# Six single PSUM banks for three double ones after the attention, and new latencies in the planner

## The chip, the cores and the metric

The kernel runs on one core of one Trainium2 chip. The metric is device time in microseconds (us) of one execution; lower is better. In the profile PE is the matrix engine (TensorE), PEld its weight loads, DVE the vector engine, ACT the scalar engine, POOL the general-purpose engine (GpSimd), and SP the engine whose queue issues most transfers. L538 is line 538 of the kernel before.

## The reference

Causal attention by blocks of 64 positions, then a feed-forward layer of two matrix products with a leaky ReLU whose slope differs by hidden channel. All data are 32-bit floats.

```python
# q, k, v: 8 batches, 8 heads, 576 positions, 64 channels
scores = scale * np.matmul(q, k.transpose(0, 1, 3, 2))
mask = block_i >= block_j                 # blocks of 64 positions
scores = np.where(mask, scores, -1000000000.0)
attn = np.exp(scores - max); attn = attn / (sum + 1e-09)
x = (attn @ v), as 4608 tokens of 512 channels
h = x @ w_in                              # 512 -> 2048
g = np.maximum(h, 0.0) + alpha * np.minimum(h, 0.0)
out = g @ w_out                           # 2048 -> 512
```

## The kernel before

**Precision.** Each 32-bit operand of the feed-forward layer is split into a high and a low part, and a product is the sum of three matmuls (high by high, low by high, high by low). The attention's matmuls take 32-bit data directly.

**Stages.** The attention goes pair by pair: a pair is two heads of one batch, 32 pairs in all. For each pair PE computes scores (L720) into PSUM, DVE takes row maxima (L725), POOL exchanges them between neighbouring groups of 32 partitions (`swap`, L697), ACT takes exponentials with their sums (L733), DVE transposes (L737), PE multiplies by v (L778), and DVE scales the result into x (L784). In between, six of the sixteen slices of hidden channels are computed for chunks of 256 tokens as they become ready (`chunk_a`): L499 is their first product, L538 their second, and partial sums go to memory. When the attention is done, the remaining ten slices are computed for nine chunks of 512 tokens. There the first product of two slices (`pair1`) is done with seven half-size products (L579) in place of eight, whose sums DVE and ACT build (L588, L592, L597). The last products (L538) add up in four accumulators per chunk, which L878 adds to the partial sums before the store. The weights of these ten slices come as 64-bit floats, or as 32-bit ones where they were converted earlier, and are prepared by DVE, ACT and POOL (L382 to L403, L419); factors of x are formed by DVE and split by ACT with DVE or POOL (L402, L403).

**A product of the first kind.** L499 is issued in three parts of four matmuls each, all into one PSUM bank; other operations can stand between the parts. L579 is issued as one operation of six matmuls into one bank. The bank is then read by ACT (L510, negated ReLU, or L597, a copy) and by DVE (L512, the leaky ReLU's other half; L588 and L592, sums, the latter back into the bank). ACT (L518) or POOL (L516) rounds the result to its high part and POOL subtracts for the low part (L521).

**PSUM.** There are eight banks of 512 floats per partition. Up to the end of the attention three tiles of two banks each, `duo`, hold scores and values, and two tiles of one bank, `bank`, serve the feed-forward work. The attention's last write of x releases an operation of the plan that closes the attention's SBUF pool (`end_attention`); its follower `more_room` then tells the planner that six more slots of the kind `bank` exist. Before the change these are the halves of the three double tiles:

```python
for i in range(2 * DUOS):
    plan.room("bank", 1, lambda slot, i=i: plan.tiles["duo"][i // 2][:, i % 2])
```

Waits between engines are put in by the framework from what each instruction reads and writes; the kernel names none.

**Order.** All work is first collected as operations with an engine, a cost, the buffers that they read and write, and a priority. `Plan.schedule` then simulates the engines: an operation is ready when its inputs are, plus the latency of the engine that made them, and each engine takes the ready operation of lowest priority number for which a buffer is free. The order that comes out is the order in which every engine's instructions are written. Its constants are costs in ns. `LAT` is added after an operation of an engine before others may use its result, `TO_POOL` is added where POOL is the user, `LONGER` stretches costs of DVE, ACT and POOL, and `LAG` shifts the priorities of the feed-forward work during the attention against those of the pairs, which are five units apart:

```python
return 5 * ((t0 + f / of) * CHA * NP / S + LAG)
```

Quotas bound how many banks serve as first products (`hp`) and accumulators (`acc`): one each during the attention, then three and two, later up to five and four.

Of the kernel before, what the change touches and what calls it, by code (L numbers as in the profile page):

```python
# [8 lines left out]
F32 = mybir.dt.float32  # L9
# [7 lines left out]
PSUM = bass.MemoryType.PSUM  # L17
# [18 lines left out]
DUOS, HB, AB, HT, AM, AT, WB = 3, 1, 1, 3, 2, 4, 4  # L36
C0, C1 = -3, 1.5
WARM, WARM_END = 10, 3400
TICK, FULL_COLUMNS, SP0 = 3413.33, 3060, 700
LAG = 7  # L40
VL = 1.0
E0, E1 = -4, 1
NEAR = 12
# [11 lines left out]
SWAP = "POOL"  # L55
# [2 lines left out]
GH, XH, XC = ("ACT", "ACT", "POOL"), "ACT", 2  # L58
LATER = ("DVE", "POOL", "DVE", "POOL", "DVE", "DVE")
GB = 6  # L60
LAT = {"PE": 110, "DVE": 145, "ACT": 135, "POOL": 20}
LONGER = 1.1
QUEUES = ("SP", "ACTQ", "POOLQ")
ISSUE, BEGINS, LANDS, PER_KB, LANES = 430, 1300, 1000, 4.1, 8
TO_POOL = 70


IN_ORDER = {"q", "k", "v", "p", "PTL", "PTH", "z", "r", "R", "raw", "m", "ef", "xb", "X", "xt", "qa", "va", "tail"}
# [16 lines left out]
class Plan:  # L85
# [16 lines left out]
    def op(self, engine, cost, fn, r=(), w=(), prio=0.0, claim=(), then=None, ends=()):  # L102

        i = len(self.ops)
        prio += SHIFTS.get(round(prio, 4), 0.0)
        deps = {j for j, o in enumerate(self.ops) if any(b.kind in ends for b in o[4])} if ends else set()
        for k in r:
            if k in self.writer:
                deps.add(self.writer[k])
        for k in w:  # L110
            if k in self.writer:
                deps.add(self.writer[k])
            deps.update(self.readers.get(k, ()))
        for k in r:
            self.readers.setdefault(k, []).append(i)
        for k in w:
            self.writer[k] = i
            self.readers[k] = []
        bufs = dict.fromkeys(k[0] if isinstance(k, tuple) else k for k in (*r, *w, *claim))
        bufs = [b for b in bufs if isinstance(b, Buf)]  # L120
        for b in bufs:
            b.users += 1
            if b.users == 1 and b.kind in IN_ORDER:
                b.after = self.last.get(b.kind)
                self.last[b.kind] = b
        deps.discard(i)
        self.ops.append((engine, cost, fn, deps, bufs, prio, then))
        return i

    def schedule(self):  # L130
# [43 lines left out]
        while events:  # L174
# [13 lines left out]
            for engine, heap in ready.items():  # L188
# [33 lines left out]
                elif engine in ("DVE", "ACT", "POOL"):  # L222
                    cost *= LONGER
                lat = LAT.get(engine, 0)
                end = t + cost
# [13 lines left out]
                for j in outs[chosen]:  # L239
                    waits[j] -= 1  # L240
                    same = self.ops[j][0] == engine == "PE"
                    more = TO_POOL if self.ops[j][0] == "POOL" else 0
                    ready_at[j] = max(ready_at[j], end + (0 if same else lat + more))
# [57 lines left out]
def attn_ffn(ctx, tc, qT, kT, vT, w_in, w_out, alpha, out):  # L301
# [30 lines left out]
    att = ExitStack()  # L332
    st = att.enter_context(tc.tile_pool(name="st", bufs=1, side="right"))
    ps = ctx.enter_context(tc.tile_pool(name="ps", bufs=1, space=PSUM))

    plan = Plan()
    op = plan.op
    pools = {}

    def rooms(pool, *kinds):  # L340
        for kind, n, shape, dt in kinds:
            plan.room(kind, n, lambda i, kind=kind, shape=shape, dt=dt: (pools[pool] if isinstance(pool, str) else pool).tile(
                [P, *shape], dt, name=f"{kind}{i}"))
# [5 lines left out]
    rooms(xring, ("tail", 1, [NCC, CHA], F32), ("xh", XC, [NCC, CHA], F32R), ("xl", XC, [NCC, CHA], F32R))  # L349
    rooms(fg, ("g", 3, [CHA], F32), ("gh", GB, [CHA], F32R),  # L350
          ("gl", GB, [CHA], F32R), ("o", 2, [DO], F32))
    rooms(ps, ("duo", DUOS, [2, 512], F32), ("bank", 8 - 2 * DUOS, [512], F32))
    plan.quota.update(hp=HB, acc=AB)
    rooms(wa, ("wa", 2 * FA, [2, 512], F32R))

# [1 line left out]
    bank = plan.tiles["bank"][0] = plan.tiles["bank"][0](0)  # L357
# [114 lines left out]
    def turn(t0, f, of):  # L472

        fseq[0] += 1
        if t0 is None:
            return 1.0e6 + fseq[0]
        return 5 * ((t0 + f / of) * CHA * NP / S + LAG)

# [208 lines left out]

    def swap(t, to, of, n, keys, key, scale, pr):

        cost = {"DVE": 75, "POOL": 290, "ACT": 150}[SWAP]  # L690

        def move(a, b):
            o, i = t()[a, to, n], t()[b, of, n]
            if SWAP == "ACT":
                nc.scalar.activation(out=o, in_=i, func=AF.Copy, scale=scale)
            else:
                (nc.vector if SWAP == "DVE" else nc.gpsimd).tensor_scalar(out=o, in0=i, scalar1=scale, scalar2=None, op0=ALU.mult)  # L697
        for i in range(4):
            a, b = slice(32 * i, 32 * i + 32), slice(32 * (i ^ 1), 32 * (i ^ 1) + 32)
            op(SWAP, cost, lambda a=a, b=b: move(a, b), r=keys, w=[(*key, i)], prio=pr)  # L700
        return [*keys, *[(*key, i) for i in range(4)]]

    def scores(src, Ts, pts, z, pr):
# [19 lines left out]
        for t, T in enumerate(Ts):  # L723
            w, o = 32 * (T + 1), off[T]
            op("DVE", c_dve(2 * w), lambda t=t, w=w, o=o: nc.vector.tensor_reduce(  # L725
                out=c()[:, 0, 2 * t:2 * t + 2], in_=sb()[:, :, o:o + w], axis=AX.X, op=ALU.max, negate=True), r=[sb], w=[(c, "n", t)], prio=pr + PM)
        keys = swap(c, 1, 0, slice(0, n), [(c, "n", t) for t in range(len(Ts))], (c, "o"), 0.125, pr + PM)
        op("DVE", 75, lambda: nc.vector.scalar_tensor_tensor(out=c()[:, 2, :n], in0=c()[:, 0, :n], scalar=0.125, in1=c()[:, 1, :n],  # L728
                                                             op0=ALU.mult, op1=ALU.min), r=keys, w=[(c, "m")], prio=pr + PM)
# [10 lines left out]
    def factors_of(z, T0, T1, pr):  # L740

        r, R = Buf("r"), Buf("R")
        ns = slice(2 * T0, 2 * T1)
        keys = swap(z, 1, 0, ns, [(z, "s", T, h) for T in range(T0, T1) for h in range(2)], (z, "o"), 1.0, pr + PZ)
        op("DVE", 80, lambda: nc.vector.scalar_tensor_tensor(out=z()[:, 2, ns], in0=z()[:, 0, ns], scalar=1e-9, in1=z()[:, 1, ns],
                                                             op0=ALU.add, op1=ALU.add), r=keys, w=[(z, "z")], prio=pr + PZ)
        if RCP:
            op("DVE", 150 + 16 * (T1 - T0), lambda: nc.vector.reciprocal(out=z()[:, 1, ns], in_=z()[:, 2, ns]), r=[(z, "z")], w=[(z, "r")], prio=pr + PZ)
        for h in range(2):
            for g in range(2):  # L750
                to, of = slice(64 * h, 64 * h + 64), slice(64 * g, 64 * g + 64)
                on = RCP[2 * h + g] if RCP else "DVE"
                fn = {"POOL": nc.gpsimd.tensor_copy, "ACT": nc.scalar.copy, "DVE": nc.vector.tensor_copy if RCP else nc.vector.reciprocal}[on]
                op(on, {"POOL": 295, "ACT": 150, "DVE": 85 if RCP else 150 + 8 * (T1 - T0)}[on], lambda h=h, g=g, to=to, of=of, fn=fn: fn(
                    out=r()[to, g, T0:T1], in_=z()[of, 1 if RCP else 2, 2 * T0 + h:2 * T1:2]), r=[(z, "r" if RCP else "z")], w=[(r, h, g)], prio=pr + PZ)
        op("DVE", 75 + 67 * (T1 - T0), lambda: nc.vector.transpose(
            out=R()[:, :, 32 * T0:32 * T1].rearrange("p g (t x) -> p g t x", x=32), in_=r()[:, :, T0:T1].unsqueeze(3).to_broadcast([P, 2, T1 - T0, 32])),
            r=[(r, h, g) for h in range(2) for g in range(2)], w=[R], prio=pr + PZ)
        return R
# [81 lines left out]
    def end_attention():  # L841
        att.close()
        pools["wb"] = ctx.enter_context(tc.tile_pool(name="wb", bufs=1, side="right"))

    def more_room():
        rooms("wb", ("w1", 3, [2, 7 * 256], F32R), ("w2", 6, [2, 512], F32R), ("xb", 1, [NCC, CHB], F32), ("X", 2, [2, 512], F32R),
              ("m", 1, [512], F32), ("ws", 1, [512], F32), ("xt", 2, [512], F32), ("g", 4, [CHA], F32))
        for i in range(2 * DUOS):
            plan.room("bank", 1, lambda slot, i=i: plan.tiles["duo"][i // 2][:, i % 2])
        plan.quota["hp"] += HT - HB  # L850
        plan.quota["acc"] += AM - AB

    op("NONE", 0, end_attention, r=xs(B - 1, (1,)), w=["att"], prio=0, then=more_room)
    later_weights(lambda f: 1000 + f)
    def more_sums():
# [71 lines left out]
```

## Time and profile before

| what | value |
|---|---|
| median of 3 runs | 1117.68 us (1116.9 to 1120.61) |
| profiled execution, its time | 1117.85 us |
| its span, first to last instruction | 1116.1 us |
| mean granted clock of PE | 0.986 |
| instructions | 32527 |
| moved by DMA | 119.56 MB, mean 107 GB/s |

A span is the time from the first instruction to the last in one profiled execution; the execution's own time is a little longer. An engine's busy time counts its instructions' durations, without waiting. Matmuls overlap each other, so their mean duration is longer than the distance between two of them. A wait is told as "engine, line, waited for: us in total, times, longest". The granted clock is 1.00 when PE runs at full speed and 0.50 when it is held at half. The profile names a half of a double tile by its tile, `duo`, and leaves buffer numbers out.

### The profile page before, as it was taken

The page shows a single profiled execution, that of the slowest core. Times are in us where ns is not written, and L with a number is a line of the kernel's source. Part 1 is how long each engine was busy: PE and PEld are TensorE (multiplying, and loading weights), DVE is VectorE, ACT ScalarE, POOL GpSimd, SP SyncE. Part 2 cuts the span into 40 slices and gives each one's busy share as a digit, 9 for nine tenths or more (in the row PEclk, how much of TensorE's full clock was granted, in tenths as well). Part 3 has the DMA queues.
Part 4 walks back from the last instruction along what each step waited for, and adds up shares of the span by engine and source line. Part 5 has one row for each costly group of instructions (what it writes and reads, how often), then busy time and mean ns, then how long its engine had stood idle before and what let it go on. Part 6 is the DMA issues. An engine that isn't in the chain of part 4 may idle for free.

```text
span 1116.1 us, 32527 instructions
## 1 busy us (share of the span) xinstructions
PE 1032.5 (93%) x12860; PEld 874.6 (78%) x12860; DVE 762.6 (68%) x1674; ACT 597.1 (53%) x2124; POOL 570.9 (51%) x1018
## 2 busy tenths in 40 slices
PE   6668999999999999999888989999999999999998
PEld 4456777877888888887777878878888888888887
DVE  6998878878777878668766974546555645464452
ACT  6877677767677667565544543324243434343331
POOL 5886545554645556559784763324242424242421
PEclk9988999999999999999899999999999999999999
DMA  9653545546354552324322122121212121212021
GB/s 299 188 173 125 172 161 155 173 152 195 133 168 159 173 160 88 127 80 147 106 95 58 39 77 75 38 76 39 76 38 77 38 76 39 76 38 76 1 76 39
DMA packets 66890, 119.56 MB, mean 107 GB/s; under 512 B 10288, under 2 KB 31024, under 8 KB 66736
## 3 DMA queue, kind: packets, MB, share of 16 engines
q1 hardware_dynamic: 66304, 117.20, 32.1%
q8 instruction: 101, 1.65, 0.6%
q14 instruction: 53, 0.43, 0.1%
q10 hardware_dynamic: 432, 0.27, 0.1%
HBM read 87.04 MB, written 29.36 MB: 104 GB/s over the span
## 4 chain that ended last, share of the span: by engine, by line
PE 71%; DVE 13%; ACT 6%; POOL 5%; issue 4%; DMA 0%; ACTq 0%; DVEq 0%; POOLq 0%
PE duo L538 15%; PE bank L538 14%; PE duo L579 12%; PE bank L499 9%; PE duo L778 7%; PE duo L720 7%; PE bank L579 4%; DVE g L512 3%; PE duo L499 3%; ACT g L510 2%; ACT p L733 2%; DVE duo L592 2%; DVE g L588 1%; DVE c L725 1%; POOL m L397 1%
## 5 line engine op out<-in xcount | busy, mean ns | idle before, releaser
L521 POOL TENSOR_TENSOR gl<-g,gh 128x256 fp32r<-128x256 f32 x288 | 232.2, 810 | 341.2 <-ACT gh L518 292.4
L733 ACT ACTIVATE p<-duo,c 128x256 f32<-128x256 f32 (+8 forms) x576 | 220.2, 408 | 32.8 <-DVE c L728 32.4
L579 PEld LDWEIGHTS duo<-X,w 128*128 128x128 f32 x1332 | 180.4, 190 | 37.4 <-DVE g L588 6.0
L579 PE MATMUL duo<-X,w 128*128 128x256 f32 x1332 | 193.7, 286 | 13.8 <-DVE g L588 4.8
L538 PE MATMUL duo<-w,gh 128*128 128x512 f32 x560 | 178.6, 400 | 10.5 <-DVE g L512 5.5
L518 ACT CAST gh<-g 128x256 fp32r<-128x256 f32 x252 | 101.8, 407 | 134.1 <-PE duo L538 78.5
L697 POOL TENSOR_SCALAR c<-c 32x4 f32<-32x4 f32 (+3 forms) x400 | 97.1, 243 | 93.2 <-DVE c L725 55.3
L725 DVE TENSOR_REDUCE c<-duo 128x2 f32<-128x512 f32 (+8 forms) x288 | 124.9, 479 | 21.1 <-PE duo L720 20.7
L733 ACT ACTIVATION_READ_ACCUMULATOR p<-duo,c 128x1 f32 x576 | 126.2, 219 | 0.0
L538 PE MATMUL bank<-wa,gh 128*128 128x512 f32 x372 | 121.8, 409 | 2.4 <-POOL wa L403 1.1
L499 PE MATMUL bank<-xh,wa 128*128 128x256 f32 x680 | 103.5, 292 | 15.0 <-DVE g L512 7.6
L499 PEld LDWEIGHTS bank<-xh,wa 128*128 128x128 f32 x680 | 89.9, 190 | 34.6 <-DVE g L512 13.9
L538 PEld LDWEIGHTS duo<-w,gh 128*128 128x128 f32 x560 | 92.8, 188 | 29.1 <-DVE g L512 10.3
L592 DVE TENSOR_TENSOR duo<-duo,g 128x256 f32<-128x256 f32 x124 | 52.6, 428 | 89.0 <-PE duo L579 82.1
L737 DVE STREAM_TRANSPOSE PTH<-p 128x576 f32<-128x576 f32 (+4 forms) x160 | 99.1, 630 | 20.6 <-ACT p L733 19.1
L510 ACT ACTIVATE g<-duo 128x256 f32<-128x256 f32 x147 | 55.8, 384 | 104.3 <-DVE duo L592 82.2
L538 PE MATMUL duo<-w,gl 128*128 128x512 f32 x280 | 110.4, 394 | 0.0
L512 DVE SCALAR_TENSOR_TENSOR g<-g,oal,duo 128x256 f32<-128x256 f32 x147 | 69.3, 476 | 51.3 <-ACT g L510 19.8
L510 ACT ACTIVATE g<-bank 128x256 f32<-128x256 f32 x141 | 54.2, 385 | 79.0 <-PE bank L499 52.5
L720 PE MATMUL duo<-k,q 64*32 64x288 f32 (+4 forms) x2560 | 84.4, 372 | 11.3 <-ACT p L733 9.1
L512 DVE SCALAR_TENSOR_TENSOR g<-g,oal,bank 128x256 f32<-128x256 f32 x141 | 66.1, 471 | 28.1 <-ACT g L510 26.8
L579 PEld LDWEIGHTS bank<-X,w 128*128 128x128 f32 x558 | 76.9, 190 | 5.6 <-DVE X L403 0.2
(87 smaller groups left out, 1833.4 us busy)
## 6 DMA issues: line engine op xcount, KB each, us to landing
v<-in_v SPq DMA_DIRECT2D x32, 576.0 KB, 4.0
k<-in_k SPq DMA_DIRECT2D x32, 288.0 KB, 4.2
xb<-xd SPq DMA_DIRECT2D x9, 1024.0 KB, 5.4
m<-part SPq DMA_DIRECT2D x36, 256.0 KB, 3.3
out<-m SPq DMA_DIRECT2D x35, 256.0 KB, 2.1
va<-in_v SPq DMA_DIRECT2D x32, 256.0 KB, 4.8
raw<-in_w_in SPq DMA_DIRECT2D x16, 512.0 KB, 3.6
raw<-in_w_out SPq DMA_DIRECT2D x16, 512.0 KB, 3.9
```

The lines of the kernel that those rows point to most:

```text
L499: nc.tensor.matmul(hp()[:, :n], ww()[:, 0, cc * P:(cc + 1) * P], x()[:, cc, :n], start=(i == 0 and cc == 0), stop=(i == 2 and cc == NCC - 1))
L510: op("ACT", c_act(CHA), lambda: nc.scalar.activation(out=g(), in_=hp()[:, ts], func=AF.Relu, scale=-1.0), r=[hp], w=[g], prio=FP)
L512: op("DVE", c_dve(CHA) + 60, lambda: nc.vector.scalar_tensor_tensor(out=g(), in0=g(), scalar=oal[:, f:f + 1], in1=hp()[:, ts], op0=ALU.mul ...
L518: op("ACT", c_act(CHA, True), lambda: nc.scalar.copy(out=gh(), in_=g()), r=[g], w=[gh], prio=FP)
L521: op("POOL", c_pool(CHA) + 60, lambda: nc.gpsimd.tensor_tensor(out=gl(), in0=g(), in1=gh().bitcast(F32), op=ALU.subtract), r=[g, gh], w=[g ...
L538: nc.tensor.matmul(acc(), a()[:, ts], ww(), start=(first and i == 0), stop=(last and i == 2))
L579: nc.tensor.matmul(bank()[:, :CHA], W()[:, i, 256 * at + P * c:256 * at + P * c + P], B()[:, j, CHA * c:CHA * c + CHA], start=(n == 0), st ...
L697: (nc.vector if SWAP == "DVE" else nc.gpsimd).tensor_scalar(out=o, in0=i, scalar1=scale, scalar2=None, op0=ALU.mult)
L720: nc.tensor.matmul(sb()[32 * i:32 * i + 32, h, off[T]:off[T] + w], q()[hs, qs], blocks(k()[hs], T + 1, 32 * (i % 2)), start=True, stop=True)
L725: op("DVE", c_dve(2 * w), lambda t=t, w=w, o=o: nc.vector.tensor_reduce(out=c()[:, 0, 2 * t:2 * t + 2], in_=sb()[:, :, o:o + w], axis=AX.X ...
L733: op("ACT", 237 + w / 1.2, lambda x=2 * t + h, T=T, h=h, w=w, o=o: nc.scalar.activation(out=pb()[:, 2 * o + h * w:2 * o + h * w + w], in_= ...
L737: op("DVE", 85 + 2.08 * w, lambda to=to, a=a, w=w, o=o: nc.vector.transpose(out=to()[:, a:a + 2 * w], in_=pb()[:, 2 * o:2 * o + 2 * w]), r ...
```

## The change

The pool of PSUM tiles is split: the three double tiles get a pool of their own, `duos`, that is closed together with the attention's SBUF pool. At that point a new PSUM pool, `banks`, is opened, from which the planner's six further `bank` slots are allocated as tiles of one bank each. The number of slots and their kind stay. Beside that, constants of the planner change: the latencies, the stretch, the cost of a swap on POOL, and `LAG`.

```diff
--- before.py
+++ after.py
@@ -37,7 +37,7 @@
 C0, C1 = -3, 1.5
 WARM, WARM_END = 10, 3400
 TICK, FULL_COLUMNS, SP0 = 3413.33, 3060, 700
-LAG = 7
+LAG = 7.25
 VL = 1.0
 E0, E1 = -4, 1
 NEAR = 12
@@ -58,11 +58,11 @@
 GH, XH, XC = ("ACT", "ACT", "POOL"), "ACT", 2
 LATER = ("DVE", "POOL", "DVE", "POOL", "DVE", "DVE")
 GB = 6
-LAT = {"PE": 110, "DVE": 145, "ACT": 135, "POOL": 20}
-LONGER = 1.1
+LAT = {"PE": 240, "DVE": 140, "ACT": 137, "POOL": 95}
+LONGER = 1.06
 QUEUES = ("SP", "ACTQ", "POOLQ")
 ISSUE, BEGINS, LANDS, PER_KB, LANES = 430, 1300, 1000, 4.1, 8
-TO_POOL = 70
+TO_POOL = 85
 
 
 IN_ORDER = {"q", "k", "v", "p", "PTL", "PTH", "z", "r", "R", "raw", "m", "ef", "xb", "X", "xt", "qa", "va", "tail"}
@@ -332,6 +332,7 @@
     att = ExitStack()
     st = att.enter_context(tc.tile_pool(name="st", bufs=1, side="right"))
     ps = ctx.enter_context(tc.tile_pool(name="ps", bufs=1, space=PSUM))
+    duos = att.enter_context(tc.tile_pool(name="duos", bufs=1, space=PSUM))
 
     plan = Plan()
     op = plan.op
@@ -349,7 +350,8 @@
     rooms(xring, ("tail", 1, [NCC, CHA], F32), ("xh", XC, [NCC, CHA], F32R), ("xl", XC, [NCC, CHA], F32R))
     rooms(fg, ("g", 3, [CHA], F32), ("gh", GB, [CHA], F32R),
           ("gl", GB, [CHA], F32R), ("o", 2, [DO], F32))
-    rooms(ps, ("duo", DUOS, [2, 512], F32), ("bank", 8 - 2 * DUOS, [512], F32))
+    rooms(ps, ("bank", 8 - 2 * DUOS, [512], F32))
+    rooms(duos, ("duo", DUOS, [2, 512], F32))
     plan.quota.update(hp=HB, acc=AB)
     rooms(wa, ("wa", 2 * FA, [2, 512], F32R))
 
@@ -687,7 +689,7 @@
 
     def swap(t, to, of, n, keys, key, scale, pr):
 
-        cost = {"DVE": 75, "POOL": 290, "ACT": 150}[SWAP]
+        cost = {"DVE": 75, "POOL": 258, "ACT": 150}[SWAP]
 
         def move(a, b):
             o, i = t()[a, to, n], t()[b, of, n]
@@ -841,12 +843,12 @@
     def end_attention():
         att.close()
         pools["wb"] = ctx.enter_context(tc.tile_pool(name="wb", bufs=1, side="right"))
+        pools["banks"] = ctx.enter_context(tc.tile_pool(name="banks", bufs=1, space=PSUM))
 
     def more_room():
         rooms("wb", ("w1", 3, [2, 7 * 256], F32R), ("w2", 6, [2, 512], F32R), ("xb", 1, [NCC, CHB], F32), ("X", 2, [2, 512], F32R),
               ("m", 1, [512], F32), ("ws", 1, [512], F32), ("xt", 2, [512], F32), ("g", 4, [CHA], F32))
-        for i in range(2 * DUOS):
-            plan.room("bank", 1, lambda slot, i=i: plan.tiles["duo"][i // 2][:, i % 2])
+        rooms("banks", ("bank", 2 * DUOS, [512], F32))
         plan.quota["hp"] += HT - HB
         plan.quota["acc"] += AM - AB
 
```

## The prediction

> **What bounds the kernel now.** I read the page's busy shares first, then the chain of work that ended last, then a table of busy time by stage, then TensorE's groups and its waits after the attention, and last a few microseconds of the timeline.
>
> ```profile
> span 1116.1 us, 32527 instructions
> PE 1032.5 (93%) x12860; PEld 874.6 (78%) x12860; DVE 762.6 (68%) x1674; ACT 597.1 (53%) x2124; POOL 570.9 (51%) x1018
> PE 71%; DVE 13%; ACT 6%; POOL 5%; issue 4%; DMA 0%; ACTq 0%; DVEq 0%; POOLq 0%
> ```
>
> TensorE (PE) is the bound: 93% busy and 71% of the final chain. No transfer is on the chain. The stages differ, so here is the same account by stage; the columns are the stage's length, then busy time and count of PE, weight loads, DVE, ACT and POOL, then the granted clock.
>
> ```profile
> 0.00:101.00 101.00, 67.88 (x1552) 50.78 (x1553) 89.64 (x223) 72.88 (x298) 75.03 (x149) 0.90 0.62 199
> 101.00:495.50 394.50, 382.69 (x7837) 320.26 (x7836) 309.00 (x753) 282.05 (x1239) 211.91 (x566) 1.00 0.46 149
> 495.50:600.00 104.50, 91.31 (x530) 78.66 (x528) 71.20 (x93) 53.05 (x114) 79.70 (x79) 0.97 0.35 114
> 600.00:660.00 60.00, 54.11 (x333) 48.06 (x334) 52.99 (x93) 30.50 (x72) 41.46 (x39) 0.97 0.22 71
> 660.00:1116.10 456.10, 436.49 (x2615) 376.87 (x2613) 239.75 (x517) 158.58 (x403) 162.81 (x187) 1.00 0.16 54
> ```
>
> The attention ends near 495.5 us; until then the double tiles hold scores and values. From there to the end all PSUM banks serve the feed-forward products, six of them as halves of the three old double tiles. In those 620.6 us PE is idle 38.7 us (620.6 minus 91.31, 54.11 and 436.49). The groups of that stretch say where (last columns: busy us, mean ns of one | idle before):
>
> ```profile
> L579 PE MATMUL duo<-X,w 128*128 128x256 f32 x1332 | 193.7, 286 | 13.8 <-DVE g L588 4.8 <-ACT g L510 2.8 <-DVE g L512 1.8
> L538 PE MATMUL duo<-w,gh 128*128 128x512 f32 x560 | 178.6, 400 | 10.5 <-DVE g L512 5.5 <-ACT g L510 2.7 <-DVE duo L592 0.9
> L579 PE MATMUL bank<-X,w 128*128 128x256 f32 x558 | 80.6, 282 | 0.0
> L538 PE MATMUL bank<-w,gh 128*128 128x512 f32 x160 | 50.0, 393 | 0.0
> L499 PE MATMUL duo<-xh,wa 128*128 128x256 f32 x184 | 29.3, 296 | 5.9 <-ACT g L510 5.9
> L499 PE MATMUL duo<-xl,wa 128*128 128x256 f32 x92 | 16.2, 301 | 3.9 <-DVE g L512 3.9
> ```
>
> The same matmul of the same line waits 13.8 us in 1332 when it writes a half of a double tile, and 0.0 us in 558 when it writes one of the two single-bank tiles. So it is for L538 (10.5 us in 560 against 0.0 in 160). Were these waits for a bank to be read and come free, single banks would show them too. One product in the timeline tells what they are:
>
> ```profile
> 554.38 0.64 PE L499 MATMUL duo<-xh,wa 128*128 128x256 f32 x4
> ...
> 555.06 0.38 ACT L510 ACTIVATE g<-duo 128x256 f32<-128x256 f32 x1 [1.33 <-PE duo L499]
> ...
> 555.50 0.74 PE L499 MATMUL duo<-xh,wa 128*128 128x256 f32 x4 [0.47 <-ACT g L510]
> ...
> 556.43 0.47 DVE L512 SCALAR_TENSOR_TENSOR g<-g,oal,duo 128x256 f32<-128x256 f32 x1
> ...
> 556.95 0.74 PE L499 MATMUL duo<-xl,wa 128*128 128x256 f32 x4 [0.71 <-DVE g L512]
> ```
>
> A product of L499 is three parts of four matmuls into one bank. The first part ran at 554.38. The second adds to the same bank, so nothing may yet read that bank, and still it waits until ACT's L510 has read a double tile (0.47 us idle), and the third until DVE's L512 has (0.71 us). What was read can only be the other half. ACT itself had sat idle 1.33 us until the first part ended. So a wait binds the whole double tile: the two products in its halves take turns. L538 shows the same: it adds up into an accumulator, and L510 and L512 never read one.
>
> **The change, part by part.** (1) Six single-bank tiles take the place of the halves: count of tiles, their slots in the planner and all products stay; what goes is the waiting between two halves. PE's waits by stage, as idle us, times, longest; first 495.5 to 600 us:
>
> ```profile
> PE duo L499 <- ACT g L510: 5.9, 9, 2.0
> PE duo L499 <- DVE g L512: 3.9, 6, 0.7
> ...
> PE duo L538 <- DVE g L512: 0.8, 1, 0.8
> ```
>
> then 600 to 660 us:
>
> ```profile
> PE duo L579 <- DVE g L588: 3.0, 3, 1.7
> ...
> PE duo L579 <- DVE duo L592: 1.0, 1, 1.0
> PE duo L579 <- DVE g L512: 1.0, 2, 0.8
> PE duo L579 <- ACT g L510: 0.7, 1, 0.7
> ```
>
> and 660 us to the end:
>
> ```profile
> PE duo L538 <- DVE g L512: 5.5, 10, 1.0
> PE duo L538 <- ACT g L510: 2.7, 6, 0.9
> PE duo L579 <- ACT g L510: 2.0, 7, 0.3
> PE duo L579 <- DVE g L588: 1.8, 3, 0.8
> PE duo L538 <- DVE duo L592: 0.9, 1, 0.9
> PE duo L579 <- DVE g L512: 0.8, 4, 0.2
> ...
> PE duo L538 <- DVE g L588: 0.4, 1, 0.4
> ```
>
> Waits for weights or factors (L403) and for L878 can be the matmul's own and are left out. Idle time understates a stall, because matmuls overlap: one lasts 286 ns, but in an undisturbed run eight start within 0.95 us, one each 119 ns:
>
> ```profile
> 529.34 1.11 PE L499 MATMUL duo<-xh,wa 128*128 128x256 f32 x8
> 530.29 0.64 PE L499 MATMUL duo<-xl,wa 128*128 128x256 f32 x4
> ```
>
> So each wait costs its idle time and 286 minus 119 = 0.167 us more (taken the same for L538, an estimate). By stage: 10.6 us in 16 waits, +2.7 = 13.3 us; 5.7 us in 7, +1.2 = 6.9 us; 14.1 us in 32, +5.3 = 19.4 us. The ceiling is 39.6 us.
>
> What is late next? From 660 us on DVE is busy 239.75 of 456.10 us, POOL and ACT about 160: none needs the time, and I take the whole 19.4. In the first stage PE's floor is its own work; POOL, at 79.70 us, still fits in 104.5 minus 13.3 = 91.2 us. I take the whole 13.3. From 600 to 660 us DVE is busy 52.99 us, and 60 minus 6.9 is 53.1: there DVE (weights and factors of the second part) is late next, at 100%. I take half, 3.4 us, between 0 and 6.9. Sum 36.1 us.
>
> A clock effect hangs on the first stage. A row of the table over a narrower stretch:
>
> ```profile
> 538.50:545.30 6.80, 6.16 (x24) 5.58 (x25) 3.46 (x8) 3.46 (x8) 4.27 (x7) 0.50 0.10 39
> ```
>
> After the longest of those waits (2.0 us) the clock is 0.50 for 6.8 us, which loses up to 3.4 us. It may come back with the wait, or another sparse moment may lose it; bounds 0 and 3.4 us, and I count 0, since 600 to 660 us stays sparse. By the Trainium skill (TensorE: Matmul & The Clock Gate, "HAM oscillation") only idle gaps over some 3.4 us bring the clock down; the trace disagrees, with a drop after 2.0 us of idle between sparse matmuls. By that page's rule this gap isn't the cause, and the sum stays as it is.
>
> (2) The handover: the first matmul into each new tile waits until the double tiles are given back. Their last reader is the last L784, which the planner already awaits before it hands out the halves; what else ends with the attention is already given back at this point. I count 0; the upper bound is one wait of the longest kind above, 2.0 us; a gain is excluded, since no wait goes here.
>
> (3) The planner's numbers. PE's latency goes from 110 to 240 ns, POOL's from 20 to 95, the stretch of the other engines from 1.1 to 1.06, a swap's cost from 290 to 258, LAG from 7 to 7.25. No instruction is added; the written order of all queues changes. How near is 240? Four matmuls at 494.99 would end, at 119 ns each, at 495.47; ACT's reader of that bank begins 0.20 us later:
>
> ```profile
> 494.99 0.64 PE L499 MATMUL bank<-xl,wa 128*128 128x256 f32 x4
> ...
> 495.67 0.39 ACT L510 ACTIVATE g<-bank 128x256 f32<-128x256 f32 x1 [1.29 <-PE bank L499]
> ```
>
> That is nearer to 240 than to 110, so the plan will place readers nearer to where they run. LAG moves the feed-forward work of the attention later by 0.25 x 5 = 1.25 of a pair's 5 units; a pair takes 394.5/32 = 12.3 us, so about 3 us; PE's total work stays, and PE is the bound before and after that point: 0. What the new order brings in the attention, rows can only bound: PE's idle time there is 394.50 minus 382.69 = 11.8 us, the most it can gain. A reordering can as well open waits, so I put the same 11.8 us on the loss side. I take 0, since PE is 97% busy there. The first 101 us, with DVE at 89.64 us, have DVE's weight work as floor: I take 0 again.
>
> **Sum.** The profiled execution took 1117.85 us (span 1116.1), 0.17 us above the median of 1117.68. 1117.85 - 36.1 = 1081.75; I say 1082 us.
>
> **The rivals.** *A half comes back (C).* Without the turns of the halves a product may wait for its own bank: DVE and ACT must do L592, L510 and L512 on a bank before it is free. Against it: the single banks' 0.0 us. For it: PE will come round sooner. L579's 1890 matmuls are 45 pairs of 42; if each pair waited the 0.47 us of the timeline once, 21 us would come back: 1103 us, and with half of that 1092.
>
> *More goes (B).* The order also closes waits in the attention (11.8 us at most), the clock (3.4 us) and the other half of 600 to 660 us (3.5 us) come too: 1082 - 18.7 = 1063 us.
>
> *Nothing goes (E).* The waits are needed ones. By the Trainium skill (PSUM — Partial Sum Buffer, "PSUM bank collisions raise a hardware error") engines are to be kept apart by bank. By that rule a program that guards just so has nothing to lose by sharing a tile, and the waits shown are true ones: 1117.85, within 0.3%. The rows speak against it: no bank is shared at 555.50, and the wait is there.
>
> *Slower (D).* With PE's readers 130 ns later in the plan, the planner slips one more feed-forward block (12 matmuls, 1.43 us) ahead of a pair's scores; on the chip the scores come late, the exponentials after them, and PE runs dry for as long. In all 32 pairs that is 45.8 us: 1128 us. It decides above 36.1 + 3.4 = 39.5 us, that is from 28 of 32 pairs on. Against it: DVE has 309.00 of 394.50 us to do there and can absorb lateness.
>
> **How the numbers follow.** The likeliest case (A): the sum, give or take half of the attention's 11.8 us and the 3.4 us of the middle stage, 9.3 us, rounded outwards: 1071 to 1092 us, chance 0.62. B, 1062 to 1071: 0.15. C, 1092 to 1108: 0.13. E: 0.05. D: 0.05. The range 1064 to 1100 leaves out D, E, half of C and a fifth of B, together 0.2. 0.3% (about 3.4 us) is what a measurement of this kernel can tell from no change. Faster: A, B and C, 0.90; same: E, 0.05; slower: D, 0.05.
>
> **What would show it.** After the attention no row names duo; the L579, L538 and L499 rows on bank have idle times near 0; PE's waits for L510, L512, L588 and L592 fall from 30 us to under 5; the stretch from the attention's end to the end shrinks by some 36 us, about 20 of it behind the stage that has DVE near full. DVE from its stage near 600 us shows as what the chain waits for. The attention still ends at 495 us, give or take 6. I am wrong if that end moves by more than 12 us, if waits on bank rows take the place of those on duo, or if the clock drops in new places.

## The result, and the profile after

The changed kernel takes 0.9692 of the time before (95% interval 0.9662 to 0.9723); the medians are 1084.5 and 1117.3 us. One of the four executions behind the 1084.5 took 2452.88 us, its L581 matmuls 530 ns on average against 282 in the profile below, and does not count in the ratio. In a second comparison, whose first execution gave the profile shown here, the ratio is 0.9681 (0.9657 to 0.9705), 1082.1 against 1118.7 us. The forecast was 1082. Code lines after the change are two higher: L499, L510, L512, L538 and L579 are now L501, L512, L514, L540 and L581.

The head of the page after:

```profile
span 1079.5 us, 32550 instructions
PE 1021.1 (95%) x12860; PEld 876.8 (81%) x12860; DVE 772.0 (72%) x1674; ACT 595.1 (55%) x2124; POOL 570.6 (53%) x1018
```

PE has as many matmuls as before, with 11.4 us less busy time (a matmul that waits inside another's time counts as busy) in a span 36.6 us shorter. Its groups after the attention (486.5 us to the end; mean ns of one | idle before):

```profile
L581 PE MATMUL bank<-X,w 128*128 128x256 f32 x1890 | 261.4, 282 | 6.2 <-DVE g L514 1.5 <-DVE X L405 1.3 <-POOL w L405 1.2
L540 PE MATMUL bank<-w,gh 128*128 128x512 f32 x720 | 225.4, 394 | 0.0
...
L540 PE MATMUL bank<-wa,gl 128*128 128x512 f32 x67 | 28.8, 429 | 6.8 <-POOL gl L523 6.8
L501 PE MATMUL bank<-xl,wa 128*128 128x256 f32 x120 | 19.3, 283 | 0.0
```

No row names duo. The 720 matmuls of L540 have no idle time, where 560 on duo had 10.5 us; L501 has none. What is left is mostly of another kind: 6.8 us for POOL's low part (L523), and waits for weights and factors (L405).

To see where the time went, both profiles are cut at the same points of PE's work: its 2001st matmul, the 9390th (just after the attention), the first L579, the first of the third of nine chunks, and the end. Columns are the stretch and its length, then busy time and count of PE, weight loads, DVE, ACT and POOL, then the granted clock, the busy share of DMA and its GB/s. Before:

```profile
0.00:124.00 124.00, 89.14 (x2001) 67.97 (x2002) 106.00 (x260) 89.33 (x374) 86.86 (x174) 0.92 0.61 197
124.00:496.20 372.20, 362.14 (x7392) 303.64 (x7391) 292.77 (x717) 266.10 (x1167) 200.54 (x541) 1.00 0.45 146
496.20:593.60 97.40, 86.76 (x502) 75.09 (x501) 66.58 (x84) 46.74 (x100) 75.52 (x76) 0.96 0.36 119
593.60:703.90 110.30, 100.69 (x611) 87.14 (x610) 83.83 (x155) 54.05 (x129) 63.76 (x63) 0.98 0.21 68
703.90:1112.50 408.60, 393.76 (x2362) 340.80 (x2360) 212.71 (x459) 140.82 (x358) 144.23 (x166) 1.00 0.15 52
```

After:

```profile
0.00:124.60 124.60, 89.73 (x1998) 67.89 (x2000) 107.85 (x262) 89.85 (x375) 83.62 (x176) 0.82 0.58 196
124.60:496.40 371.80, 365.92 (x7410) 307.42 (x7392) 299.09 (x715) 265.06 (x1167) 206.94 (x545) 1.00 0.47 152
496.40:589.90 93.50, 86.47 (x504) 73.12 (x503) 67.06 (x82) 44.98 (x97) 70.80 (x71) 0.96 0.31 104
589.90:693.10 103.20, 96.98 (x611) 86.00 (x610) 84.09 (x155) 53.54 (x129) 64.92 (x62) 1.00 0.20 68
693.10:1075.20 382.10, 382.03 (x2362) 342.39 (x2360) 213.19 (x459) 141.63 (x358) 144.27 (x167) 1.00 0.16 56
```

The first two stretches are as long as before. The third lost 3.9 us, the fourth 7.1 and the last 26.5: there PE is busy 382.03 of 382.10 us, so its own work is all that is left. The clock of the first stretch is lower, 0.82 against 0.92, and its length is the same within 0.6 us.

### The profile page after: what moved, and what is told of

The parts are those of the page before. It is cut to its first block, busy times and chain, and to the rows that moved or that the text cites. A ratio compares the mean times of both kernels' runs of the same rounds, so it can differ in the third digit from the quotient of the medians.

```text
span 2451.1 us, 32550 instructions
## 1 busy us (share of the span) xinstructions
PE 2432.2 (99%) x12860; PEld 1841.5 (75%) x12860; DVE 757.0 (31%) x1674; ACT 606.6 (25%) x2124; POOL 549.0 (22%) x1018
## 4 chain that ended last, share of the span: by engine, by line
PE 98%; DVE 1%; ACT 1%; POOL 0%; issue 0%; DMA 0%; ACTq 0%; DVEq 0%; POOLq 0%
PE bank L540 42%; PE bank L581 23%; PE bank L501 16%; PE duo L780 9%; PE duo L722 8%; ACT p L735 0%; DVE c L727 0%; POOL c L699 0%; DMA qa<-in_k 0%; DVE PTL L739 0%; DVE xT L786 0%; ACT wa L404 0%; DVE ef L389 0%; DVE m L384 0%; POOL m L399 0%
## 5 line engine op out<-in xcount | busy, mean ns | idle before, releaser
L581 PEld LDWEIGHTS bank<-X,w 128*128 128x128 f32 x1890 | 602.3, 402 | 99.8 <-issue 88.0
L581 PE MATMUL bank<-X,w 128*128 128x256 f32 x1890 | 611.0, 530 | 0.0
L540 PE MATMUL bank<-w,gh 128*128 128x512 f32 x720 | 512.0, 827 | 0.0
L523 POOL TENSOR_TENSOR gl<-g,gh 128x256 fp32r<-128x256 f32 x288 | 217.7, 757 | 1115.9 <-PE bank L540 582.6
L540 PEld LDWEIGHTS bank<-w,gh 128*128 128x128 f32 x720 | 258.2, 398 | 75.9 <-issue 75.9
L540 PE MATMUL bank<-wa,gh 128*128 128x512 f32 x432 | 307.0, 829 | 1.5 <-POOL gh L518 1.5
L501 PEld LDWEIGHTS bank<-xh,wa 128*128 128x128 f32 x864 | 262.5, 406 | 56.6 <-issue 45.8
L540 PE MATMUL bank<-w,gl 128*128 128x512 f32 x360 | 298.0, 828 | 0.0
L501 PE MATMUL bank<-xh,wa 128*128 128x256 f32 x864 | 285.9, 529 | 2.8 <-ACT wa L404 2.8
L512 ACT ACTIVATE g<-bank 128x256 f32<-128x256 f32 x288 | 110.4, 383 | 705.1 <-PE bank L501 412.6
L514 DVE SCALAR_TENSOR_TENSOR g<-g,oal,bank 128x256 f32<-128x256 f32 x288 | 135.2, 477 | 349.1 <-ACT g L512 345.6
L540 PEld LDWEIGHTS bank<-wa,gh 128*128 128x128 f32 x432 | 148.7, 373 | 74.8 <-issue 68.1
L540 PEld LDWEIGHTS bank<-w,gl 128*128 128x128 f32 x360 | 126.6, 352 | 70.9 <-issue 69.8
L540 PE MATMUL bank<-wa,gl 128*128 128x512 f32 x216 | 177.0, 819 | 0.0
L780 PE MATMUL duo<-PTH,v 64*64 64x160 f32 (+4 forms) x2304 | 173.5, 532 | 0.0
```

What stands on the lines that cost most here:

```text
L501: nc.tensor.matmul(hp()[:, :n], ww()[:, 0, cc * P:(cc + 1) * P], x()[:, cc, :n], start=(i == 0 and cc == 0), stop=(i == 2 and cc == NCC - 1))
L512: op("ACT", c_act(CHA), lambda: nc.scalar.activation(out=g(), in_=hp()[:, ts], func=AF.Relu, scale=-1.0), r=[hp], w=[g], prio=FP)
L514: op("DVE", c_dve(CHA) + 60, lambda: nc.vector.scalar_tensor_tensor(out=g(), in0=g(), scalar=oal[:, f:f + 1], in1=hp()[:, ts], op0=ALU.mul ...
L523: op("POOL", c_pool(CHA) + 60, lambda: nc.gpsimd.tensor_tensor(out=gl(), in0=g(), in1=gh().bitcast(F32), op=ALU.subtract), r=[g, gh], w=[g ...
L540: nc.tensor.matmul(acc(), a()[:, ts], ww(), start=(first and i == 0), stop=(last and i == 2))
L581: nc.tensor.matmul(bank()[:, :CHA], W()[:, i, 256 * at + P * c:256 * at + P * c + P], B()[:, j, CHA * c:CHA * c + CHA], start=(n == 0), st ...
```

## The experiments

Theory H: products in the two halves of a double tile take turns, and that goes. Theory O: the planner's new order makes the gain.

**The changed kernel again (e0_after).** No edit.

> The changed kernel once more, for a profile at its usual clock. Its median stands at 1084.5 us against 1117.3 us before, 32.8 us less. Theory H (the halves): what goes is the turn-taking of two products in the halves of one double tile. Then PE's waits for L510, L512, L588 and L592 (30.4 us after the attention before the change, by the old line numbers) are under 5 us, the attention still ends at 495 us, give or take 6, and the stretch from there to the end is about 585 us in place of 620.6. Theory O (the order): the planner's new latencies make the gain. Then a good part of it lies ahead of the attention's end, which comes 10 us or more earlier, and waits of that kind stay.

Measured: 1082.1 us. Of the four named waits after the attention, 2.3 us are left by the rows (L514 1.5, L590 0.8). From the matmul just after the attention to the end it takes 578.8 us against 616.3 before (sums of the last three stretches), 37.5 less. The attention's last write of x ends at 487.6 us against 495.5 before. These 7.9 us lie outside the 6 that H gave and short of O's 10. PE's 9390th matmul still falls at 496.4 against 496.2: other work moved behind the attention.

**Tiles alone (e1_tiles_only, and once more as e11_tiles_again).** The changed kernel with the old constants; every engine's instructions stand in the order of before.

```diff
-LAG = 7.25
+LAG = 7
-LAT = {"PE": 240, "DVE": 140, "ACT": 137, "POOL": 95}
-LONGER = 1.06
+LAT = {"PE": 110, "DVE": 145, "ACT": 135, "POOL": 20}
+LONGER = 1.1
-TO_POOL = 85
+TO_POOL = 70
-        cost = {"DVE": 75, "POOL": 258, "ACT": 150}[SWAP]
+        cost = {"DVE": 75, "POOL": 290, "ACT": 150}[SWAP]
```

> The six single-bank tiles alone; all planner constants are those of before, so that every engine's instructions stand in the order of before, and only waits differ. Theory H: nearly the whole gain, 1080 to 1090 us; the attention ends at 495 us, as before. Theory O: 1114 to 1120 us. A third theory (both are needed, because the old order plans readers too early and a product then waits for its own bank): 1095 to 1108 us, with waits on rows of bank in place of those on duo.

> The six single-bank tiles alone, once more, beside the last three: 1072 to 1076 us. By the first look its last part, from the third chunk to the end, takes 382.0 us against 408.5 before; this should repeat to 0.2 us, and what varies between executions should lie in the first 130 us.

Measured: 1073.6 us, 0.9616 (0.9581 to 0.9651), and again 1074.7 us, 0.9620 (0.9593 to 0.9646). Both are below the changed kernel, and below the 1080 to 1090 us that H had for this run: the tiles give more than the whole gain. The second run, cut at the same points:

```profile
0.00:123.10 123.10, 86.19 (x2000) 65.83 (x2001) 106.73 (x260) 89.26 (x374) 86.21 (x174) 0.90 0.60 198
123.10:493.50 370.40, 361.71 (x7391) 303.91 (x7390) 292.57 (x717) 265.71 (x1167) 200.04 (x541) 1.00 0.45 147
493.50:583.60 90.10, 82.81 (x503) 71.29 (x502) 66.96 (x84) 46.05 (x100) 77.87 (x76) 1.00 0.38 129
583.60:686.00 102.40, 96.50 (x611) 86.06 (x609) 83.17 (x155) 53.79 (x129) 64.51 (x62) 1.00 0.21 68
686.00:1068.10 382.10, 382.04 (x2362) 342.42 (x2360) 212.99 (x459) 141.63 (x358) 144.00 (x167) 1.00 0.16 57
```

With the order unchanged, the three stretches after the attention give 7.3, 7.9 and 26.5 us: 41.7. The last one repeated to the tenth. What varies between executions is the start: the same order reached the 2001st matmul at 129.1 us in the first profile and at 123.1 here. PE's waits after the attention begin with:

```profile
PE bank L540 <- POOL gl L523: 6.3, 7, 1.3
PE bank L581 <- DVE w L405: 2.3, 2, 1.9
PE bank L581 <- POOL w L405: 1.7, 2, 1.1
```

**The planner's constants alone (e2_plan_only).** The kernel before with the new constants, the halves kept; the order is that of the changed kernel. The edit is the other part of the diff.

> The planner's new constants alone, with the halves of the double tiles as before; every engine's instructions stand in the order of the changed kernel. Theory H: 1112 to 1122 us, with some 30 us of waits on duo rows after the attention. Theory O: 1084 to 1092 us. If it is slower than before by more than 3 us, the new order by itself meets more turns of the halves.

Measured: 1114.6 us, 0.9976 (0.9960 to 0.9993). Its last three stretches:

```profile
498.20:604.00 105.80, 89.51 (x503) 77.53 (x502) 63.68 (x82) 45.60 (x97) 70.07 (x71) 0.94 0.27 91
604.00:712.50 108.50, 98.46 (x610) 85.75 (x609) 84.48 (x155) 53.15 (x129) 65.15 (x63) 1.00 0.20 68
712.50:1111.00 398.50, 390.77 (x2362) 341.81 (x2360) 214.14 (x460) 139.94 (x358) 144.60 (x166) 1.00 0.15 53
```

and the waits of the first of these:

```profile
PE duo L499 <- ACT g L510: 9.3, 9, 3.1
PE duo L499 <- DVE g L512: 3.9, 5, 1.3
PE duo L499 <- ACT o L650: 2.2, 1, 2.2
```

Theory O falls as the cause. The new order does do something on the halves: the last stretch is 10.1 us shorter than before, the first 8.4 longer, since more turns fall among the L499 products (15.4 us of waits against 9.8). With single banks the last stretch is 382.1 us whatever the order, so what the order won there is won by the tiles anyway, and its cost elsewhere stays.

**Other partners (e4_repaired).** The kernel before; only which two slots share a double tile differs.

```diff
-            plan.room("bank", 1, lambda slot, i=i: plan.tiles["duo"][i // 2][:, i % 2])
+            plan.room("bank", 1, lambda slot, i=i: plan.tiles["duo"][i % DUOS][:, i // DUOS])
```

> The kernel before with one edit: slot i of the six is half i // 3 of double tile i % 3, in place of half i % 2 of tile i // 2. Banks, their number, every engine's order and all planner constants are those of before; only which two slots share a tile differs. Theory H (two products in the halves of one tile take turns): neighbouring slots are taken one after the other, so keeping them apart changes which products meet; PE's idle time after the attention (38.7 us before) moves by 8 us or more, and the time with it, to 1085 to 1110 us if long-lived accumulators now sit beside each other, or to over 1125 us if each now sits beside a first product. The rival that each bank's own reuse makes the waits: no change, 1115 to 1121 us, as each bank's own history is the same.

Measured: 1107.5 us, 0.9920 (0.9890 to 0.9951), inside H's first range and outside the rival's. Number of banks, order and each bank's own use are those of before, so the bank's own reuse can't make the difference. The third and last stretches:

```profile
493.90:583.70 89.80, 83.81 (x502) 72.38 (x501) 67.86 (x84) 46.28 (x100) 78.53 (x76) 0.98 0.39 129
...
692.70:1101.50 408.80, 394.39 (x2362) 340.72 (x2361) 212.94 (x458) 140.98 (x359) 144.58 (x167) 1.00 0.15 53
```

and L499 on duo after the attention:

```profile
L499 PE MATMUL duo<-xh,wa 128*128 128x256 f32 x184 | 25.9, 283 | 1.0 <-DVE g L512 1.0
```

Neighbouring L499 products now lie in different tiles; their waits fall from 9.8 to 1.0 us and the third stretch from 97.4 to 89.8 us, as with single banks. The last stretch stays at 408.8 us, with waits of the old kind (L538 for L512: 4.3 us in 8). Presumably other pairs of accumulators and products meet there; no run separates them. PE's idle time after the attention, expected to move by 8 us or more, moved by 5.7 (from 35.1 to 29.4 us by the last three stretches), the time by 8.5. The tile as the unit of the wait is shown for L499 by this run, and for the last stretch by the tiles alone, where the same order on the same number of banks has no wait left.

**Single constants on the single-bank tiles.** Five kernels, each the changed tiles with old constants but for those named: LAG at 7 with all others new (e3), the latencies and TO_POOL (e5), LONGER and the swap (e6), LAG 7.25 (e7), LONGER (e8), the swap (e9).

```diff
+LAT = {"PE": 240, "DVE": 140, "ACT": 137, "POOL": 95}     # e5, with TO_POOL = 85
+LONGER = 1.06                                             # e8; e6 with the swap
+        cost = {"DVE": 75, "POOL": 258, "ACT": 150}[SWAP] # e9; e6
+LAG = 7.25                                                # e7
```

> The changed kernel with LAG at 7 in place of 7.25; tiles and latencies as changed. The feed-forward work of the attention is planned 1.25 units earlier, a quarter of a pair's 5 units, some 3 us. If LAG only shifts work that PE has to do anyway, the time is within 3 us of the changed kernel's. If LAG's value decides how the attention's last pairs and the first feed-forward products meet, it differs by 5 us or more, either way.

> Single-bank tiles with the new latencies (PE 240, DVE 140, ACT 137, POOL 95, and 85 more towards POOL), the other constants as before. The new constants together cost 8.5 us on top of the tiles (1082.1 against 1073.6 us). If the latencies make that: 1079 to 1084 us, with the attention's first 130 us longer or its end later. If LONGER and the swap's cost make it: 1071 to 1076 us. If only the sum of all does: between the two.

> Single-bank tiles with LONGER 1.06 and the swap at 258, the latencies and LAG as before. If these make the 8.5 us: 1079 to 1084 us. If the latencies do: 1071 to 1076 us.

> Single-bank tiles with LAG 7.25, the rest as before. With the new latencies, LAG at 7.25 in place of 7 stood 1.4 us higher (1082.1 against 1080.7 us). If LAG only shifts work: within 3 us of 1073.6 us. If it decides how the attention's end meets the following products: 5 us or more away.

> Single-bank tiles with LONGER 1.06, every other constant as before. LONGER 1.06 and the swap's 258 together stood at 1091.8 us, 18.2 us above the tiles alone (1073.6). If LONGER makes that: 1085 to 1093 us, with the lost time between the attention's last pairs and the first products of the nine chunks. If the swap does: 1072 to 1077 us.

> Single-bank tiles with the swap's cost at 258, every other constant as before. If the swap's cost makes the 18.2 us: 1085 to 1093 us. If LONGER does: 1072 to 1077 us. If neither does alone, a planned order is a chance matter of all constants, and both kernels lie within 5 us of 1073.6.

| new constants on single banks | us | of the time before (interval) |
|---|---|---|
| none (e1, e11) | 1073.6, 1074.7 | 0.9616, 0.9620 |
| latencies (e5) | 1075.6 | 0.9634 (0.9610 to 0.9658) |
| LAG (e7) | 1077.5 | 0.9649 (0.9622 to 0.9676) |
| swap (e9) | 1081.7 | 0.9678 (0.9658 to 0.9697) |
| LONGER (e8) | 1090.8 | 0.9759 (0.9737 to 0.9780) |
| LONGER and swap (e6) | 1091.8 | 0.9779 (0.9755 to 0.9804) |
| all but LAG (e3) | 1080.7 | 0.9671 (0.9642 to 0.9700) |
| all (e0) | 1082.1 | 0.9681 (0.9657 to 0.9705) |

Three of the six came out as one of their theories had it (e3, e5, e8); e6 lies above both of its ranges, e7 and e9 between theirs. LONGER costs most, some 16 us, the swap 7 and LAG 3; the latencies, which cost 1 to 2 us alone, take about 11 us back where LONGER and the swap are new (1091.8 to 1080.7). Where LONGER's time goes shows in the second and third stretch (370.4 and 90.1 us with the old value):

```profile
128.30:505.90 377.60, 367.65 (x7408) 303.81 (x7391) 290.32 (x714) 266.98 (x1164) 203.75 (x542) 1.00 0.45 146
505.90:602.40 96.50, 88.74 (x504) 76.00 (x503) 66.49 (x82) 44.73 (x98) 72.69 (x73) 0.93 0.34 113
```

Seven us lie in the attention and six behind it. Another five are in the first stretch, which varies by six between two executions of one order (129.1 and 123.1 us). Which placements do it is not settled: since orders differ, the same count of matmuls is not quite the same work.

**Less for POOL (e10_tiles_later).** Tiles alone, and one weight subtraction per pair of slices moved from POOL to DVE.

```diff
-LATER = ("DVE", "POOL", "DVE", "POOL", "DVE", "DVE")
+LATER = ("DVE", "DVE", "DVE", "POOL", "DVE", "DVE")
```

> Single-bank tiles, constants as before, and one of the two weight subtractions on POOL (LATER's second entry, 1.4 us, one for each of five pairs of slices) given to DVE. After the tiles, PE's waits between the attention's end and the first of the nine chunks are all for POOL's L523 (5.7 us in 6 waits). If POOL's load makes them: 3 us or more come back, 1066 to 1071 us. If DVE, which takes that work, is as near its limit: 1073 to 1078 us. A change of the order as a whole can hide either by 3 us.

Measured: 1071.7 us, 0.9581 (0.9558 to 0.9605), between its two ranges. It is the fastest here; against tiles alone (0.9593 to 0.9646) the intervals overlap. PE's largest wait after the attention is

```profile
PE bank L540 <- POOL gl L523: 3.1, 5, 1.6
```

halved. The third stretch takes 88.3 us against 90.1, the fourth 101.0 against 102.4. So POOL's load makes part of the waits. A gain in time is not shown: the difference of 2 to 3 us is not clear of noise, and the new order can hide as much.

## Why the prediction was right

The time, 1084.5 and 1082.1 us against 1082, is inside the range, and the mechanism was right: e1 and e4 show it. Two terms were mis-sized, one by 5.6 us and one by 7.4 to 8.5 us the other way. That they nearly cancel, and the time was met so closely, is luck.

**Turns of the halves, 36.1 us predicted, 41.7 measured** (e11 against before, same order). Here is e11, cut at the matmuls that stood at 495.7, 600.1 and 660 us before, where the stages were 104.4, 59.9 and 456.1 us long:

```profile
493.00:587.50 94.50, 86.76 (x529) 74.70 (x529) 69.59 (x87) 50.21 (x109) 80.00 (x78) 1.00 0.38 126
587.50:645.50 58.00, 52.55 (x336) 46.63 (x335) 54.48 (x98) 33.24 (x80) 44.07 (x41) 1.00 0.21 73
645.50:1071.70 426.20, 422.54 (x2615) 378.81 (x2613) 239.85 (x516) 158.50 (x401) 162.72 (x187) 1.00 0.17 58
```

Since both kernels issue the same matmuls in the same order, the start of each can also be compared with that of the one before it.

- 495.5 to 600 us: 13.3 predicted, 9.9 measured. Starts that were late before give back 20.0 us (a time at half clock among them), and new late starts take 10.0 of it. The step that failed is "PE's floor is its own work", with "POOL ... still fits": a busy share said that POOL had room, but L523 has to come right behind its own product, and PE now waits 6.3 us for it. It is rival C's form, a wait that takes the place, with POOL in the part that C gave to DVE and ACT.
- 600 to 660 us: half of 6.9, 3.4 predicted; 1.9 measured. The limit seen there was real. DVE is busy 54.48 of the 58.00 us, not all of them, and PE's waits are for weights and factors (L405): 3.6 us for DVE's and 2.1 for POOL's.
- From there on: 19.4 predicted, 29.9 measured, the term that was furthest off. 44 starts with idle time before them gain 23.0 us: 15.9 of idle time and 0.16 us each, as estimated. Of that idle time the sum had 14.1 us, because the list of waits leaves out the shortest and the sum left out those for L878. Another 69 starts gain 7.1 us, some 0.1 us each, without any idle time before them: a delay shorter than the overlap of two matmuls leaves none. All 113 write duo before.

**The planner's numbers, 0 predicted with 11.8 us either way.** On single banks they cost 7.4 to 8.5 us (1082.1 against 1074.7 and 1073.6), on halves they gain 0.24%. That is inside the bounds, but the reason given for 0 ("PE is 97% busy there") fails: 4.2 us of the loss lie behind the attention (93.5 and 103.2 us against e11's 90.1 and 102.4), in stretches that the bound left out. LAG, put at 0, stood at 1.4 to 3.9 us. "Nearer to where they run" is true of a reader's latency and no measure of time: e5, with the latencies alone, is no faster than e1.

**The handover, 0 predicted.** In the changed kernel's timeline PE goes from the last values (ended 486.4 us) into the next products without an idle row; the longest gap is 0.15 us, at 487.72 us, just after the last write of x. e11's list has no wait for L786.

**The clock, 0 counted.** The 6.8 us at half speed that followed a wait are gone in e11 (clock 1.00 in the third stretch, 0.96 before) and have their like in the changed kernel (0.96). In e1, the same kernel as e11, that stretch has 0.98 and is no longer, 89.9 against 90.1 us, so a gain by the clock does not show.

**The signs.** Of the three signs of being wrong, the end of the attention moved by 7.9 us, less than 12 but more than the 6 allowed. Waits of another kind stand on bank rows now (L523, 6.8 us), far less than the 30 us that went. The clock did drop in new places, in the first stretch above all, and that stretch is 0.6 us longer.

**The rivals.** E falls with e1 and e4, and with it the use made there of a rule of the Trainium skill (PSUM — Partial Sum Buffer, "PSUM bank collisions raise a hardware error"): keeping engines apart by bank needs no wait between two halves, and the runs agree, with 0.0 us of idle on 720 matmuls beside readers of other banks. The program before waited by tile, which is more than that rule asks. B and D did not come: the stretch of the attention is 371.8 us against 372.2, where B had up to 11.8 less and D 45.8 more.

## What to carry to other kernels

Where two buffers share one tile, look for waits of a kind that a single-buffer tile of the same line does not have; a wait in the middle of one accumulation is the clearest sign here. Splitting the tile cost nothing here and needed no new order. A planner whose numbers are brought nearer to the trace need not plan a faster order: test the numbers alone and one by one, on the kernel that they will run in, since what they gained on the halves was gone once the tiles were apart.

## What the runs showed of the hardware that was not expected

The clock fell to half after a wait shorter than the 3.4 us for which it then stayed down. In the changed kernel, PE's timeline and the stretch after it:

```profile
546.24 0.49 PE L540 MATMUL bank<-wa,gl 128*128 128x512 f32 x1 [2.21 <-POOL gl L523]
```

```profile
543.40:546.80 3.40, 1.19 (x4) 0.68 (x5) 2.96 (x6) 3.04 (x8) 2.68 (x3) 1.00 0.42 148
546.80:550.20 3.40, 3.40 (x10) 2.61 (x9) 3.40 (x4) 1.35 (x2) 3.40 (x4) 0.50 0.36 137
```

A stretch with PE busy 1.19 of 3.40 us is followed by one at 0.50. In the traces here the recorded clock changes only at steps of 3.41 us. Cut at these steps, the waits of 0.88 and 1.27 us that e11 has at the end of that part of the work lie in two stretches, and brought no drop:

```profile
554.15:557.57 3.42, 2.30 (x10) 1.25 (x8) 3.42 (x7) 1.92 (x6) 3.42 (x5) 1.00 0.08 18
557.57:560.98 3.41, 2.37 (x10) 1.96 (x11) 3.25 (x6) 1.23 (x3) 3.41 (x4) 1.00 0.61 220
```

The same holds in all thirteen traces that have clock records, from 30 us on. Of the stretches at full clock, the 57 with PE busy under 1.61 us were all followed by half clock, of 73 with 1.61 to 2.03 us 28 were, and of 3722 with more none. The longest idle time inside one of the 57 was between 0.88 and 3.23 us, so the busy share of such a stretch fits and the length of one gap does not. The rule of the Trainium skill (TensorE: Matmul & The Clock Gate, "HAM oscillation"), no idle gaps over some 3.4 us, is thus not enough to keep the clock up here.
